# Inverse FFT with its twiddle in the last stage's tables, a 64-bit conversion on three engines, and spare banks for the first batch

## The chip, the cores and the metric

The kernel runs on one core of a Trainium2 chip. The metric is the device time of one execution in microseconds; the median of three runs is given. Beside it there is one profiled execution, whose trace gives the time of every instruction on the engines: PE (TensorE, matmuls; its weight loads are shown as PEld), DVE (VectorE), ACT (ScalarE), POOL (GpSimd) and SP (SyncE). SP, ACT and POOL also issue DMAs, each in a queue of its own that works in order.

## What is computed

A block of two layers, in float32 and float64 on the host; x is (8, 3072, 256).

```python
X = np.fft.rfft(x, axis=1)                        # along the sequence
Yr = Xr @ w_r - Xi @ w_i + b_r                    # complex mixing, 256 x 256
Yi = Xr @ w_i + Xi @ w_r + b_i
Yr = np.sign(Yr) * np.maximum(np.abs(Yr) - 0.01, 0.0)   # Yi likewise
y = np.fft.irfft(Yr + 1j * Yi, n=3072, axis=1)    # (8, 3072, 256)
h = y.reshape(-1, 256) @ w_in                     # 256 -> 2048
g = h * np.tanh(np.log1p(np.exp(np.minimum(h, 20.0))))  # Mish
out = g @ w_out                                   # 2048 -> 256
```

`w_in` and `w_out` come as float64. Nearly every matrix is split into a high and a low part, and a product is made of three matmuls: high by high, low by high, high by low.

## The kernel before

Each batch goes through a chain of four stages, which `chain` (L690) lists as segments of items; between the stages the data lie in DRAM scratch (`scratch`, L310: `s1`, `s3`, `s2`).

- Stage a (`item_a`, 13 items): loads x, splits it, multiplies with the constant table `fa`, forms sum and difference of two halves on DVE into a tile `ev` and stores it to `s1`. The store is issued from ACT's queue (L353).
- Stage b/m (12 blocks; `item_b`, then `item_m`): a block loads 256 KB from `s1` (L365) and a table `tt`, finishes the forward transform (`psb`), splits the result into `xh` and `xl`, multiplies it with the mixing weights (`psm` in the first batch; `psk` and `psp` in the others), thresholds it on DVE (L447) and stores `y` to `s3`. For blocks 0 to 10 a matmul of 256 columns gives two halves, which an ACT copy (`cor`, L414) and a DVE addition (`xf`, L415) add up, in two banks one after the other.
- Stage c (`item_c`, 13 items): loads rows of `s3` in four DMAs of 60 KB, two of them from POOL's queue (`get2`, L582), splits them, multiplies by the inverse transform of length 12 with its twiddle factors, which differ from group to group: 26 tables in seven loads of 450 KB a batch (`cload`, L597). Six matmuls of 256 columns, one ACT copy, a store to `s2` from ACT's queue.
- Stage f (`item_f`, 12 items, two to each chunk of 512 columns): loads 256 KB of `s2` in two DMAs of 64 rows (L657), multiplies by the constant table `vv`, adds, and leaves `yh` and `yl` for the FFN.

The FFN works through 48 chunks with 16 steps each: `ffn1` (L748, six matmuls into `hp`, then Mish on ACT), `split_g` (L763, on DVE for two steps at once: `gh`, `gl`) and, four steps behind (`LAG`), `ffn2` (L771, twelve matmuls into two accumulators `acc`). The chain of batch b+1 is woven into the FFN of batch b: the loop at L868 makes one FFN step and then lets `run_chain` make one step of the chain, or of an f item of the present batch (L884). The first batch has no FFN beside it: its chain runs alone (L844), and only the conversion of the weights runs with it.

That conversion (`from_double`, L224) turns 64-bit numbers into a high and a low part: 16 jobs (`SetupWin`, `SetupWout`) of 512 KB each. A job has nine steps, five tensor_scalars and two scalar_tensor_tensors on DVE, a copy on ACT, and two additions, on POOL in the first half of the start and on DVE later (`aux_eng`). `aux_steps` puts them between the items: 14 jobs ahead of the FFN, two (`N_LATE`) in its first steps.

The order of the work is the order in which the program writes it. `run_chain` (L705) loads `la` items ahead, prepares (splits) `pla` items ahead and then calls the item's matmuls. Buffers come from pools in turn: four load tiles (and, in the first batch, four more of `p_h`), two `ev` tiles, two 4 KB tiles for tables in `p_t`. The eight banks of PSUM are two for `hp`, two for everything in the chain (`ps_d`) and four for the accumulators (`ps_o`).

Of the kernel before, what the change touches and what calls it, by code (L numbers as in the profile page):

```python
# [18 lines left out]
SEQ = 3072  # L19
# [8 lines left out]
def _dft_constants():  # L28
# [42 lines left out]
    u = np.zeros((26, 120, 120))  # L71
    b = np.arange(12)
    for g in range(26):
        nj = 5 if g < 25 else 2
        for j in range(nj):
            k1 = 5 * g + j + 1
            for k2 in range(12):
                th = ang(k1 + 256 * k2, b)
# [7 lines left out]
    cr, ci = 48 + 2 * b, 48 + 2 * b + 1  # L86
    for k2 in range(6):
        th = ang(128 + 256 * k2, b)
        u[25, 48 + 2 * k2, ci], u[25, 49 + 2 * k2, ci] = 2 * np.cos(th), -2 * np.sin(th)
        if k2 < 5:  # L90
            th = ang(256 * (k2 + 1), b)
            u[25, 60 + 2 * k2, cr], u[25, 61 + 2 * k2, cr] = 2 * np.cos(th), -2 * np.sin(th)
    u[25, 70, cr] = np.where(b % 2, -1.0, 1.0)
    u[25, 71, cr] = 1.0

    v = np.zeros((2, 64, 2, 128))
    aa = np.arange(128)
    for s in range(127):
        th = 2.0 * np.pi * (((s + 1) * aa) % 256) / 256
        v[0, s // 2, s % 2], v[1, s // 2, s % 2] = 2 * np.cos(th) / n, -2 * np.sin(th) / n  # L100
    v[0, 63, 1], v[1, 63, 1] = 1.0 / n, np.where(aa % 2, -1.0, 1.0) / n
    v = v.reshape(128, 2, 128)
# [12 lines left out]
def constants():  # L115
# [5 lines left out]
    u = np.concatenate([u, np.zeros((2,) + u.shape[1:], np.float32)])  # L121
    u = u.reshape(7, 4, 120, 2, 120).transpose(0, 2, 1, 3, 4)
    v = np.stack(_hi_lo(v), 2)
# [4 lines left out]
def fft_mix_ffn_kernel(ctx: ExitStack, tc: tile.TileContext, x, w_r, w_i, b_r, b_i, w_in, w_out,  # L128
# [10 lines left out]
    p_t = ctx.enter_context(tc.tile_pool(name="p_t", bufs=2))  # L139
    p_y = ctx.enter_context(tc.tile_pool(name="p_y", bufs=2))  # L140
    p_h = ctx.enter_context(tc.tile_pool(name="p_h", bufs=4))
# [9 lines left out]
    vv = const.tile([128, 2, 2, 128], F32R, name="vv")  # L151
# [9 lines left out]
    u_scr = dramc.tile([7, 120, 4, 2, 120], F32, name="u_scr")  # L161
# [4 lines left out]
    n_ld = [0]  # L166

    def ld_tile(b=1):
        n_ld[0] += 1
        if b == 0 and n_ld[0] % 2:  # L170
            return p_h.tile([128, 512], F32, tag="h", name="ldh")
        return p_ld.tile([128, 512], F32, tag="ld", name="ld")

# [18 lines left out]

    mixraw = []
# [18 lines left out]
    def setup_v():  # L212
        nc.gpsimd.dma_start(out=vv, in_=c_v)

    def copy_consts(n):

        if n < 11:
            nc.sync.dma_start(out=t_scr[n], in_=c_t[n])
        else:
            nc.sync.dma_start(out=t0_scr, in_=c_t0)  # L220
        if n < 7:
            nc.sync.dma_start(out=u_scr[n], in_=c_u[n])

    def from_double(raw, hi, lo, two, t):  # L224


        rv = raw.bitcast(I32).rearrange("p a f -> p (a f)")
        words = rv.rearrange("p (k c w) -> p k c w" if two else "p (c w) -> p c w", w=2, **({"k": 2} if two else {}))
        low, high = (words[:, :, :, n] if two else words[:, :, n] for n in range(2))
        cc = f32(high)  # L230
        if two:
            t = t.rearrange("p (k c) -> p k c", k=2)
        ti = t.bitcast(I32)
        nc.vector.tensor_scalar(out=ti, in0=high, scalar1=0x7FFFFFFF, scalar2=None, op0=ALU.bitwise_and)
        yield
        nc.vector.tensor_scalar(out=t, in0=t, scalar1=E_MIN, scalar2=E_MAX, op0=ALU.max, op1=ALU.min)
        yield
        nc.vector.tensor_scalar(out=ti, in0=ti, scalar1=4, scalar2=1,
                                op0=ALU.logical_shift_left, op1=ALU.logical_shift_right)
        yield  # L240
        nc.vector.tensor_scalar(out=ti, in0=ti, scalar1=0x40000000, scalar2=None, op0=ALU.bitwise_xor)
        yield
        nc.vector.scalar_tensor_tensor(out=ti, in0=high, scalar=-0x80000000, in1=ti,
                                       op0=ALU.bitwise_and, op1=ALU.bitwise_or)
        nc.scalar.activation(out=hi, in_=t, func=ACTF.Copy)
        yield
        nc.vector.tensor_scalar(out=high, in0=ti, scalar1=-0x800000, scalar2=None, op0=ALU.bitwise_and)
        yield
        nc.vector.scalar_tensor_tensor(out=cc, in0=cc, scalar=2.0 ** -52, in1=low.bitcast(U32),
                                       op0=ALU.mult, op1=ALU.mult)  # L250
        yield
        eng = aux_eng[0]
        eng.tensor_tensor(out=t, in0=t, in1=f32(hi), op=ALU.subtract)
        yield
        eng.tensor_tensor(out=lo, in0=cc, in1=t, op=ALU.add)
        yield

    aux_eng = [nc.gpsimd]

    def dt_tile(n):  # L260
        if n is None:
            return p_z.tile([128, 512], F32, tag="y", name="dt")
        return p_y.tile([128, 2, 512], F32, tag=("yh", "yl")[n % 2], name="dt")[:, 0, :]

    N_LATE = 2

    def late(n):
        return n >= 8 - N_LATE

    def raw_tile(n):  # L270
        if n >= 8:
# [657 lines left out]
```

## Time and profile before

| | |
|---|---|
| median of three runs | 2962.04 us (2954.77 to 2965.49) |
| the profiled execution | 2962.3 us, its span 2960.5 us |
| PE busy | 2780.4 us, 94% |
| DVE busy | 1898.4 us, 64% |
| ACT busy | 950.3 us, 32% |
| POOL busy | 171.8 us, 6% |
| mean granted clock of PE | 0.977 |
| DMA | 273.88 MB, 93 GB/s |

Shares are of the span. Busy time of an engine counts the time in which at least one of its instructions runs; issuing a DMA is not counted. A wait in the list of waits reads "engine, tile, line <- what ended the wait: us in total, times, the longest". In the chain of waits a row is a start, a length and what the time went to; a row that names a DMA is a transfer for which somebody waited. In a group of instructions the numbers behind the bar are busy us and the mean ns of one.

### The profile page before, as it was taken

What the parts mean: (1) busy time and instruction counts of PE and PEld (TensorE: products, weight loads), DVE (VectorE), ACT (ScalarE), POOL (GpSimd) and SP (SyncE); (2) the same over time, 40 slices, a digit from 0 to 9 for tenths busy, and PEclk for the clock granted to TensorE, in tenths of its full rate; (3) what the DMA queues carried; (4) which work ended last, traced back from release to release, by engine and by line L of the source; (5) the groups of instructions that cost most, each with busy time, mean ns of one, the idle gap of its engine ahead of it and who ended that gap; (6) DMA issues with size and microseconds to landing.
All of it is one profiled execution on the core that took longest, in us unless ns stands there. A gap on an engine that the chain in (4) does not pass through costs nothing.

```text
span 2960.5 us, 47048 instructions
## 1 busy us (share of the span) xinstructions
PE 2780.4 (94%) x18344; PEld 2549.5 (86%) x18344; DVE 1898.4 (64%) x3222; ACT 950.3 (32%) x1914; POOL 171.8 (6%) x268
## 2 busy tenths in 40 slices
PE   2647999999999999999999999999999999999999
PEld 2536899988999899998999989998999889999998
DVE  4667676566765677566765677656775667654443
ACT  2223333323333333323333233333333233332222
POOL 1230001000020000100010000100002000100000
PEclk9967999999999999999999999999999999999999
DMA  5474233432242322522234322423225222330000
GB/s 157 119 178 138 92 111 103 117 101 72 78 120 81 113 68 61 156 82 78 82 90 123 101 75 75 120 83 109 70 60 162 82 73 82 92 110 29 15 26 15
DMA packets 189399, 273.88 MB, mean 93 GB/s; under 512 B 27711, under 2 KB 114963, under 8 KB 188873
## 3 DMA queue, kind: packets, MB, share of 16 engines
q1 hardware_dynamic: 129745, 190.32, 21.1%
q10 hardware_dynamic: 40088, 50.34, 5.7%
q0 software_dynamic: 19344, 30.21, 4.1%
q8 instruction: 144, 2.36, 0.3%
q14 instruction: 78, 0.64, 0.1%
HBM read 170.03 MB, written 107.31 MB: 94 GB/s over the span
## 4 chain that ended last, share of the span: by engine, by line
PE 83%; DMA 8%; DVE 5%; issue 2%; SPq 1%; ACT 1%; ACTq 0%; DVEq 0%
PE acc L784 34%; PE hp L756 33%; DMA ld<-s 5%; PE psp L493 4%; PE psc L631 2%; PE psf L675 2%; PE psk L474 2%; PE psa L346 2%; PE psb L409 2%; DMA s<-ev 1%; PE psm L510 1%; DMA ld<-in_x_dram 1%; DVE lo L179 1%; PE psf L676 1%; PE psb L411 1%
## 5 line engine op out<-in xcount | busy, mean ns | idle before, releaser
L784 PE MATMUL acc<-wout,gh 128*128 128x256 f32 x6144 | 1144.4, 285 | 0.0
L756 PE MATMUL hp<-yh,win 128*128 128x512 f32 x3072 | 1090.4, 395 | 3.2 <-ACT yh L684 3.2
L784 PEld LDWEIGHTS acc<-wout,gh 128*128 128x128 f32 x6144 | 964.9, 190 | 20.3
L761 ACT ACTIVATE s<-hp 128x512 f32<-128x512 f32 x768 | 459.0, 598 | 1508.6 <-PE hp L756 1351.3
L784 PE MATMUL acc<-wout,gl 128*128 128x256 f32 x3072 | 871.9, 284 | 0.0
L756 PEld LDWEIGHTS hp<-yh,win 128*128 128x128 f32 x3072 | 582.8, 190 | 102.6 <-ACT yh L684 3.4
L756 PE MATMUL hp<-yl,win 128*128 128x512 f32 x1536 | 607.4, 395 | 0.0
L784 PEld LDWEIGHTS acc<-wout,gl 128*128 128x128 f32 x3072 | 582.7, 190 | 0.0
L768 DVE TENSOR_TENSOR gl<-s,gh 128x1024 fp32r<-128x1024 f32 x384 | 472.5, 1230 | 65.1 <-PE acc L784 29.3
L767 DVE CAST gh<-s 128x1024 fp32r<-128x1024 f32 x384 | 264.6, 689 | 324.2 <-ACT s L761 324.1
L756 PEld LDWEIGHTS hp<-yl,win 128*128 128x128 f32 x1536 | 291.5, 190 | 36.0 <-DVE yl L685 0.4
L179 DVE TENSOR_TENSOR lo<-ld,hi 128x512 fp32r<-128x512 f32 (+3 forms) x383 | 263.4, 688 | 46.4 <-ACT hi L178 31.8
L585 POOL DMA_DIRECT2D ld<-s x184 | 109.7, 605 | 2066.6 <-DMA ld<-s 1233.6
L176 DVE CAST hi<-ld 128x512 fp32r<-128x512 f32 (+3 forms) x362 | 150.3, 415 | 83.7 <-DMA ld<-s 62.2
L679 DVE TENSOR_TENSOR eo<-psf,cor 128x256 f32<-128x256 f32 x192 | 77.4, 422 | 173.8 <-ACT cor L678 173.0
L675 PE MATMUL psf<-vv,hi 128*128 128x256 f32 x384 | 100.2, 333 | 43.9 <-DVE sm L433 21.0
L631 PE MATMUL psc<-hi,uu 120*120 120x256 f32 (+1 forms) x416 | 100.7, 303 | 38.3 <-ACT ev L633 26.2
L346 PE MATMUL psa<-hi,fa 120*120 120x256 f32 (+1 forms) x416 | 100.8, 303 | 35.0 <-DVE ev L351 25.1
L493 PE MATMUL psp<-wmix,xh 128*128 128x256 f32 x672 | 133.1, 282 | 0.0
L675 PEld LDWEIGHTS psf<-vv,hi 128*128 128x128 f32 x384 | 74.0, 193 | 53.1 <-ACT s L761 21.8
L448 DVE TENSOR_TENSOR y<-psp,y 128x512 f32<-128x512 f32 x84 | 58.0, 690 | 92.7 <-PE psp L493 92.7
L631 PEld LDWEIGHTS psc<-hi,uu 120*120 120x120 f32 (+1 forms) x416 | 74.4, 196 | 46.4 <-ACT ev L633 29.3
(106 smaller groups left out, 2685.7 us busy)
## 6 DMA issues: line engine op xcount, KB each, us to landing
s<-ev ACTq DMA_DIRECT2D x192, 240.0 KB
out_dram<-ot SPq DMA_DIRECT2D x48, 512.0 KB
ld<-s SPq DMA_DIRECT2D x90, 256.0 KB
ld<-s SPq DMA_DIRECT2D x180, 128.0 KB
s<-y SPq DMA_DIRECT2D x352, 64.0 KB
uu<-u_scr SPq DMA_DIRECT2D x49, 450.0 KB
ld<-in_x_dram SPq DMA_DIRECT2D x180, 120.0 KB
tt<-t_scr SPq DMA_DIRECT2D x66, 256.0 KB
```

Source lines behind the costliest of these rows:

```text
L176: nc.vector.tensor_copy(out=hi, in_=src)
L179: nc.vector.tensor_tensor(out=lo, in0=src, in1=f32(hi), op=ALU.subtract)
L346: nc.tensor.matmul(out=ps[:K, sl], lhsT=fa[:K, h, s, :K], rhs=m[:K, sl], start=n == 0, stop=n == 2)
L493: nc.tensor.matmul(out=it.ps[:, ri * 256:(ri + 1) * 256], lhsT=m[:, c, 130 - ri * 128:258 - ri * 128], rhs=wmix[:, c, s, 2 * ri, :], start ...
L585: eng.dma_start(out=t[p:p + n, g * 256:(g + 1) * 256], in_=rows(k, nrow))
L631: nc.tensor.matmul(out=ps[sl], lhsT=u_t[pr // 2][:K, 2 * (pr % 2) + g, s, :K], rhs=m[sl], start=n == 0, stop=n == 2)
L675: nc.tensor.matmul(out=ps[:, p], lhsT=it.hi[:, q:q + 128], rhs=vv[:, p], start=True, stop=False)
L756: nc.tensor.matmul(out=hp, lhsT=win[:, k, s, f * 128:(f + 1) * 128], rhs=m[:, k, :], start=n == 0, stop=n == 5)
L761: nc.scalar.activation(out=s_t[t // 2][:, t % 2, :], in_=hp, func=ACTF.Mish)
L767: nc.vector.tensor_copy(out=gh, in_=s)
L768: nc.vector.tensor_tensor(out=gl, in0=s, in1=f32(gh), op=ALU.subtract)
L784: nc.tensor.matmul(out=p, lhsT=m[:, t % 2, o:o + 128], rhs=wout[:, f, s, :], start=f == 0 and h == 0 and n == 0, stop=last and h == 1 and ...
```

## The change

1. The twiddle factors of the inverse transform move from the tables of stage c to those of stage f. Stage c then has one table for all groups (three variants, `uu`, loaded once), its groups take rows in steps of two so that an item is one block of 512 columns, and three matmuls of 512 columns take the place of six of 256. Stage f has a table of its own for each item (`it.v`, 256 KB, 12 a batch), loaded by `cload`. `s3` is laid out with even and odd rows apart and `s2` like `s1`; an f item's load is one DMA and all four loads of a c item go through SP's queue.
2. The conversion is cut into three parts. DVE has five operations a job (one in `first`, four in `second`), ACT two copies, POOL the clamp of the exponent, a subtraction, a multiplication and an addition. Ten jobs instead of 14 lie ahead of the FFN, six in its first 17 steps, two program steps in each.
3. The first batch takes its load tiles, `ev` tiles and banks in turn from pools that the FFN uses later (`ld_tile`, `ev_tile`, `ps_tile`), while `started` is false: seven load tiles, five `ev` tiles, all eight banks. In the first batch blocks 0 to 10 of stage b add three matmuls of 128 columns into one bank, as block 11 did, and need no `cor` and no `xf`.
4. In all batches `ps_d` has three banks and `ps_o` three, tables have four tiles of 2 KB, and the `s1` store of stage a goes from ACT's queue to SP's.

```diff
+    uu = const.tile([120, 3, 2, 120], F32R, name="uu")
-    ps_d = ctx.enter_context(tc.tile_pool(name="ps_d", bufs=2, space=PSUM))
-    ps_o = ctx.enter_context(tc.tile_pool(name="ps_o", bufs=4, space=PSUM))
+    ps_d = ctx.enter_context(tc.tile_pool(name="ps_d", bufs=3, space=PSUM))
+    ps_o = ctx.enter_context(tc.tile_pool(name="ps_o", bufs=3, space=PSUM))
...
+    def ld_tile():
+        if not started[0] and turn("ld", 7) in (1, 3, 5):
+            return p_s.tile([128, 2, 512], F32, tag="s", name="lds")[:, 0, :]
         return p_ld.tile([128, 512], F32, tag="ld", name="ld")
+    def ev_tile():
+        if not started[0] and turn("ev", 5) in (1, 2, 4):
+            return p_g.tile([128, 2, 512], F32, tag="gh", name="evg")[:, 0, :]
+        return p_ev.tile([128, 512], F32, tag="ev", name="ev")
+    def ps_tile(name):
+        k = 0 if started[0] else turn("ps", 8)
+        if k in (1, 4, 7):
+            return ps_o.tile([128, 512], F32, tag="o", name=name)
+        if k in (2, 5):
+            return ps_h.tile([128, 512], F32, tag="h", name=name)
+        return ps_d.tile([128, 512], F32, tag="d", name=name)
...
+        def first(self):
+            self.t = p_dt.tile([128, 2, 256], F32, tag="dt", name="dt")
+            nc.vector.tensor_scalar(out=self.t.bitcast(I32), in0=self.high, scalar1=0x7FFFFFFF, scalar2=None,
+                                    op0=ALU.bitwise_and)
+            nc.gpsimd.tensor_scalar(out=self.t, in0=self.t, scalar1=E_MIN, scalar2=E_MAX, op0=ALU.max, op1=ALU.min)
+        def second(self):
...
+            nc.vector.tensor_scalar(out=ti, in0=ti, scalar1=4, scalar2=1,
+                                    op0=ALU.logical_shift_left, op1=ALU.logical_shift_right)
+            yield
+            nc.vector.tensor_scalar(out=ti, in0=ti, scalar1=0x40000000, scalar2=None, op0=ALU.bitwise_xor)
+            yield
+            nc.vector.scalar_tensor_tensor(out=ti, in0=high, scalar=-0x80000000, in1=ti,
+                                           op0=ALU.bitwise_and, op1=ALU.bitwise_or)
+            yield
+            nc.vector.tensor_scalar(out=high, in0=ti, scalar1=-0x800000, scalar2=None, op0=ALU.bitwise_and)
+            yield
+        def third(self):
+            cc, lowf = f32(self.high), f32(self.low)
+            nc.scalar.activation(out=self.hi, in_=self.t, func=ACTF.Copy)
+            nc.scalar.activation(out=lowf, in_=self.low.bitcast(U32), func=ACTF.Copy, scale=2.0 ** -52)
+            nc.gpsimd.tensor_tensor(out=self.t, in0=self.t, in1=f32(self.hi), op=ALU.subtract)
+            nc.gpsimd.tensor_tensor(out=cc, in0=cc, in1=lowf, op=ALU.mult)
+            nc.gpsimd.tensor_tensor(out=self.lo, in0=cc, in1=self.t, op=ALU.add)
+    N_EARLY = 10
...
-            nc.scalar.dma_start(out=s1[5 * pr:5 * pr + J].rearrange("j m c -> (j m) c"), in_=ev[:K])
+            nc.sync.dma_start(out=s1[5 * pr:5 * pr + J].rearrange("j m c -> (j m) c"), in_=ev[:K])
...
-            if blk == 11:
-                ps = ps_d.tile([128, 2, 256], F32, tag="d", name="psb")
+            if blk == 11 or b == 0:
+                ps = ps_tile("psb").rearrange("p (c i) -> p c i", c=2)
...
+                                nc.tensor.matmul(out=ps[:, c].rearrange("p (r e i) -> p e r i", r=2, e=2)[:, e],
+                                                 lhsT=m[:, o:o + 128],
+                                                 rhs=it.tt[0][:, e, s].rearrange("p (r i) -> p r i", r=2),
+                                                 start=n == 0, stop=n == 5)
...
+            ps = ps_tile("psc")
+            for g in range(1 if pr < 12 else 2):
+                sl = slice(0, 512) if pr < 12 else slice(g * 256, (g + 1) * 256)
+                var = 0 if pr < 12 else 1 + g
                 for n, (s, m) in enumerate(((0, it.hi), (0, it.lo), (1, it.hi))):
-                    nc.tensor.matmul(out=ps[sl], lhsT=u_t[pr // 2][:K, 2 * (pr % 2) + g, s, :K], rhs=m[sl], start=n == 0, stop=n == 2)
+                    nc.tensor.matmul(out=ps[:K, sl], lhsT=uu[:K, var, s, :K], rhs=m[:K, sl], start=n == 0, stop=n == 2)
...
-            for ri in range(2):
-                nc.sync.dma_start(out=it.t[64 * ri:64 * ri + 64].rearrange("q (p c) -> q p c", p=2),
-                                  in_=s2[:, 2 * nb + ri, :].rearrange("(q p) c -> q p c", p=2))
+            nc.sync.dma_start(out=it.t, in_=s2.rearrange("q m c -> m q c")[2 * nb:2 * nb + 2])
+        def cload():
+            it.v = p_t.tile([128, 2, 2, 128], F32R, tag="t", name="vt")
+            if b == 0:
+                nc.gpsimd.dma_start(out=it.v, in_=c_v[nb])
+            else:
+                nc.sync.dma_start(out=f32(it.v), in_=v_scr[nb])
...
-        segs.append([item_c(b, p) for p in (*range(8), 12, *range(8, 12))])
+        segs.append([item_c(b, p) for p in (12, *range(12))])
...
+        PACE = (1, 0.6, 1, 3)
-        for k in run_chain(first, la=6, cla=4, on_seg=on_seg):
+        for k in run_chain(first, la=6, cla=3, on_seg=on_seg):
...
-            if 1 <= t <= 15:
-                aux_steps(3)
+            if t < 17:
+                aux_steps(2)
```

`PACE` is the number of conversion steps for each step of the chain, by segment. At the borders of the segments three, five and eight steps are made at once.

More of the change, by code (lines that the diff above doesn't have):

```diff
@@ L191, in setup_dft, with setup_u @@
         nc.gpsimd.dma_start(out=fa, in_=c_fa)
+    def setup_u():
+        nc.gpsimd.dma_start(out=uu, in_=c_u)
     mixraw = []
@@ L220, in copy_consts @@
             nc.sync.dma_start(out=t0_scr, in_=c_t0)
[L221 to L256, printed above, removed]
@@ new lines, in fft_mix_ffn_kernel, with weight_jobs, w1, w2 @@
+    N_EARLY = 10
+    def weight_jobs():
+        def w1(k, n):
+            sl = slice(n * 512, (n + 1) * 512)
+            return (w_in.bitcast(I32)[k * 128:(k + 1) * 128, n * 1024:(n + 1) * 1024],
+                    *(win[:, k, s, sl].rearrange("p (a c) -> p a c", a=2) for s in range(2)), False)
+        def w2(n):
+            return (w_out.bitcast(I32)[n * 256:(n + 1) * 256, :].rearrange("(k p) c -> p k c", p=128),
+                    *(wout[:, 2 * n:2 * n + 2, s, :] for s in range(2)), True)
+        order = [w1(0, 0), w1(1, 0), w1(0, 1), w1(1, 1), w2(0), w2(1), w1(0, 2), w1(1, 2), w2(2), w2(3),
+                 w1(0, 3), w1(1, 3), w2(4), w2(5), w2(6), w2(7)]
+        return [FromDouble(n, *a) for n, a in enumerate(order)]
@@ L341, in mm @@
         def mm():
-            ps = ps_d.tile([128, 512], F32, tag="d", name="psa")
+            ps = ps_tile("psa")
             for h in range(2):
@@ L359, in item_b @@
         it = Item()
+        it.tt = []
         def load():
[L362 removed]
+            it.t = ld_tile()
             s1 = scratch(b)[0]
@@ L504, in mm_c @@
             if c == 0:
-                it.ps = ps_d.tile([128, 512], F32, tag="d", name="psm")
+                it.ps = ps_tile("psm")
             xh, xl = src.x
@@ L800, in fft_mix_ffn_kernel @@
         setup_dft()
-        aux = [SetupWin(k, n) for n in range(4) for k in range(2)] + [SetupWout(n) for n in range(8)]
+        aux = weight_jobs()
         n_raw = [0]
@@ L808, in aux_load @@
                 n_raw[0] += 1
-        N_EARLY = len(aux) - N_LATE
         def aux_run():
+            aux_load(3)
+            aux[0].first()
+            yield
             for n, job in enumerate(aux):
-                aux_load(n + 1)
-                for _ in job.work():
-                    yield n
-                aux_load(min(n + 4, N_EARLY) if n < N_EARLY else n + 4)
+                if n:
+                    aux[n - 1].third()
+                aux_load(n + (3 if n + 3 > N_EARLY else 4))
+                yield from job.second()
+                if n + 1 < len(aux):
+                    aux[n + 1].first()
+                yield
+            aux[-1].third()
         aux_gen = aux_run()
         n_aux = [0]
-        started = [False]
         def aux_steps(m):
             for _ in range(m):
-                if n_aux[0] < 9 * (len(aux) if started[0] else N_EARLY):
+                if started[0] or n_aux[0] < 5 * N_EARLY + 2:
                     next(aux_gen, None)
```

275 lines of the change are left out of this document (101 added, 174 removed).

## The prediction

> **What bounds the kernel now.** I read the page first, then busy time in windows cut at the stage borders of the first batch, then the waits of PE, then the chain of waits and the time line inside each stage.
>
> ```profile
> span 2960.5 us, 47048 instructions
> ...
> PE 2780.4 (94%) x18344; PEld 2549.5 (86%) x18344; DVE 1898.4 (64%) x3222; ACT 950.3 (32%) x1914; POOL 171.8 (6%) x268
> ```
>
> ```profile
> 0.00:63.05 63.05, 20.89 (x78) 17.19 (x78) 27.91 (x56) 16.65 (x34) 10.86 (x18) 1.00 0.52 163
> 63.05:172.73 109.68, 61.31 (x250) 48.66 (x250) 71.63 (x139) 27.65 (x58) 26.06 (x29) 0.93 0.45 123
> 172.73:233.38 60.65, 22.16 (x78) 17.53 (x78) 33.98 (x63) 19.38 (x35) 18.60 (x31) 0.50 0.74 190
> 233.38:245.17 11.79, 4.31 (x17) 3.64 (x17) 5.09 (x12) 3.87 (x9) 0.00 (x0) 0.50 0.40 126
> 245.17:275.72 30.55, 24.13 (x117) 20.10 (x118) 28.50 (x46) 8.51 (x16) 6.60 (x6) 0.84 0.33 100
> 275.72:2700.00 2424.28, 2391.91 (x16145) 2209.16 (x16145) 1619.69 (x2762) 803.92 (x1639) 109.63 (x185) 0.99 0.32 94
> 2700.00:2960.50 260.50, 255.67 (x1663) 233.23 (x1661) 111.60 (x150) 70.28 (x125) 0.00 (x0) 1.00 0.06 20
> ```
>
> The columns of the windows are length, busy time (and instructions) of PE, PEld, DVE, ACT and POOL, granted clock, DMA share, GB/s. The borders are the first b load (63.05), the first c load (172.73), the first f load (233.38), the first FFN matmul (245.17), and the end of the last long PE gap of the start (275.72). From there PE is the bound: 2391.91 of 2424.28 busy, 32.4 us idle. Before it lie 245 us in which the first batch has the chip alone and PE works 109 of them, and 30.6 us in which the FFN starts while DVE is busy 28.50. So a change to the steady part can win at most the 32.4 us and what it takes off PE; the larger store is the 275.7 us.
>
> The profiled execution took 2962.3 us, its span 2960.5, so 1.8 us lie around it; the median of the runs is 2962.04. I sum against 2962.3.
>
> **Steady part.** PE's waits from 276 us on are all of one kind:
>
> ```profile
> PE psf L675 <- DVE sm L433: 21.0, 7, 3.0
> PE psf L675 <- DVE ev L351: 7.5, 6, 1.5
> ```
>
> An f item takes two banks of `ps_d`, which has two. When a b item of block 11 (it keeps its bank until `sm` is made) or an a item (until `ev`) stands before it, the second `psf` waits for that bank. With three banks the second `psf` finds one free: 21.0 + 7.5 = 28.5 us are at stake. What is late next in f is its own `lo`, the rest of the 32.4. I take 25 off; ends: 32 (all), 10 (if PE only runs into the next bank). The bank comes from the output accumulators, which go from four to three: a chunk then takes its second bank from the previous chunk's first accumulator. ACT copies that right behind its last matmul, and between lie the other accumulator, an FFN1 step and one more accumulator: about 0.7 + 1.4 + 0.7 us of matmuls by the rows below. I cost it at 0; if ACT came 2 us later in each of 47 changes of chunk, half of that would be lost.
>
> ```profile
> 282.52 1.39 PE hp L756 x6
> 283.91 0.71 PE psa L346 x6
> 284.62 1.43 PE acc L784 x12
> ```
>
> The c items' six matmuls of 256 columns become three of 512. Six of 256 take 0.71 us, three of 512 half of 1.39, so 0.02 us for twelve items in seven batches: 2 us. Wider matmuls and half the weight loads bring no more, since the weight loads are hidden. The tables are an exchange: 7 of 450 KB for u against 12 of 256 KB for v in each batch.
>
> ```profile
> 202.28 0.69 SPq L580
> ...
> 234.03 2.60 DMA ldh<-s
> ```
>
> SP takes more: the `s1` stores come from ACT's queue (ACT, and the Mish behind, no longer wait there for `ev`, but PE didn't wait for that), and the c loads that POOL issued. The next x load now stands behind a store that waits for `ev`. An x item has two loads to issue, at some 0.7 us (SPq, above), and a step of the loop lasts 1.39 + 0.71 + 1.43 = 3.5 us, so the queue keeps up but runs less far ahead; who waits then is `hi` on DVE, with `gh` and `gl` of the FFN behind it. FFN2 runs four steps behind FFN1, some 7 us of slack after the cast. I take +4 for all batches, ends 0 and +20.
>
> **The conversion.**
>
> ```profile
> L768 DVE TENSOR_TENSOR gl<-s,gh 128x1024 fp32r<-128x1024 f32 x384 | 472.5, 1230 | 65.1 <-PE acc L784 29.3 <-PE hp L756 0.9
> ...
> L243 DVE SCALAR_TENSOR_TENSOR dt<-raw,dt 128x512 int32<-128x512 int32 x16 | 11.1, 692 | 0.5
> ...
> L253 POOL TENSOR_TENSOR dt<-dt,win 128x512 f32<-128x512 f32 x8 | 10.1, 1266 | 99.5 <-ACT win L245 99.5
> ...
> L238 DVE TENSOR_SCALAR dt<-dt 128x512 int32<-128x512 int32 x16 | 6.9, 431 | 0.5
> ```
>
> ```profile
> 251.31 1.29 POOL L253 TENSOR_TENSOR dt<-dt,wout 128x512 f32<-128x512 f32 x1 [26.42 <-ACT wout L245]
> 251.47 2.21 DVE L768 TENSOR_TENSOR gl<-s,gh 128x1024 fp32r<-128x1024 f32 x1
> ```
>
> A job costs DVE five tensor_scalars like L238 and two operations like L243 now, 5 x 0.43 + 2 x 0.69 = 3.5 us, 4.9 where two more are on DVE. After: 4 x 0.43 + 0.69 = 2.4 in five steps (0.48 each); ACT gets one more copy; POOL gets four operations, three like L253 (1.27) and a clamp that no row shows; the nearest are L238 on DVE (0.43) and L253 itself, and I take 1.3: 5.1 us a job on POOL. And POOL's operations hold DVE up: `gl` took 2.21 beside POOL's 1.29, against 1.23.
>
> **The first batch, stage by stage.**
>
> ```profile
> 34.61 5.04 DMA s<-ev
> ...
> 53.03 4.99 DMA s<-ev
> ```
>
> Stage a: from 34 us on the chain goes through stores of `ev`, the first and the last of three shown, because a third item needs one of two tiles back. With five tiles and eight banks in turn these waits go. Next is the DMA: 63.05 us at 163 GB/s are 10.3 MB, and at 190, the rate of stage c, they take 54 us. The store joins SP behind two more loads, where it delays nothing that isn't already six ahead. 63 to 53: -10; ends -4 and -18.
>
> Stage b/m: the chain goes from one block's `psm` over DVE to the next one's. The first, and two neighbours later:
>
> ```profile
> 84.90 4.67 PE psm L510 x12
> ...
> 134.18 3.06 PE psm L510 x12
> ...
> 140.93 3.06 PE psm L510 x12
> ```
>
> `psm` and two `psb` in turn share two banks, so PE waits for DVE and DVE for PE, 6.75 us a block, 3.7 of them outside `psm`. After the change `psb` is one bank without the ACT copy and the two `xf` adds, and eight banks in turn uncouple the two engines. PE needs 3.06 plus twelve matmuls of 128 columns, no longer than the twelve of `acc` (1.43): 4.5 us. DVE needs `lo`, `xl` and a threshold of two operations and a clamp, priced like L243 (0.69, the same 128x512) and L238 (0.43), and 1.8 steps of conversion (0.6 for each of three yields, at 0.48): 4 x 0.69 + 0.43 + 0.87 = 4.1. With up to 0.8 of hold by POOL it is 4.9. But the b load has a price of its own:
>
> ```profile
> 69.80 5.00 SPq L365 DMA_DIRECT2D ldh<-s  x1
> ```
>
> ```profile
> 70.00:80.00 10.00, 4.38 (x15) 3.56 (x16) 1.99 (x3) 2.04 (x5) 0.00 (x0) 1.00 0.14 53
> ```
>
> While only b loads run, 256 KB take 5.0 us at 53 GB/s with a DMA share of 0.14, about two of 16 engines. Twelve of them can't come faster, and tables, raw weights and stores share those two. So 5.0 is one end of a block and 6.75, as now, the other; I take 5.5, nearer to 5.0 because the loads run three ahead. From first load to first `psm` 22 us as now (63 to 85), eleven blocks of 5.5, a tail of 6: 88 against 109.7, -21; ends -8 and -30.
>
> Stage c: all four loads of an item go to SP.
>
> ```profile
> uu<-in_c_u_dram POOLq DMA_DIRECT2D x7, 450.0 KB, 8.4
> ```
>
> 13 x 4 issues of 0.7 are 36 us, and behind the last come its landing (2.6 as the f load's, above), split, matmuls and copy (some 3) and the last store (up to 5.0 as in stage a): 47. By bytes: 60.65 us at 190 GB/s are 11.5 MB; without 3.15 MB of u tables 8.4 MB, 44 us. So 49, above both, against 60.7: -12; ends -6 and -17.
>
> Stage f: now two DMAs an item, which land in 2.60 us (above). The new single one, (2 rows m, 64 q, 512) into 128 partitions, has word for word the form of the b load, so I price it at 5.0 us and the second behind the first at 10: +5; ends 0 and +8. In the Trainium skill, "DMA: Bandwidth & Descriptors", section "Why a DMA increments its semaphore by 16 and not by 1", the number of engines is the largest up to 16 that divides the slowest dimensions of both sides: 128 and 2 here, so two engines. The trace agrees (share 0.14); without the row I would, by that rule alone, come to the same +5, and by size alone to 0.
>
> **The FFN's opening.** In the stages ahead of the FFN the conversion is covered by the waits above. But 10 instead of 14 jobs come before the FFN, so six instead of two fall into its first 15 steps. There DVE has no room: 28.50 of 30.55 now. Six jobs add 6 x 2.4 = 14 us, and 24 operations at 0 to 1.0 us of hold add 0 to 24. In the steady window DVE is busy 1619.69 of 2424.28, so a third of a step's 3.5 us is free; with the a splits that fall here I take 0.9 us, 13 over 15 steps; a lag of 5 is hidden by FFN2's distance. With half the holds (12): 14 + 12 - 13 - 5 = 8, to be set against the two jobs whose cost is in today's 30.55 and which partly stay. I take +10 for the opening; ends 0 and, with every hold and no lag hidden, 14 + 24 - 13 = +25.
>
> The Trainium skill, "SBUF — State Buffer", section "Who interferes with whom", says that of a DVE operation with two SBUF inputs and a reading GpSimd one the second blocks fully until the first ends. The rows agree (0.98 us lost behind 1.29). By the rule taken strictly, every one of the 24 would block and the opening cost the +25.
>
> **Sum.** a -10, b/m -21, c -12, f +5, opening +10, `psf` waits -25, c columns -2, SP and DMA in the steady part +4: -51. 2962.3 - 51 = 2911. Its own range, with single terms between their ends: 2897 to 2927.
>
> **The rivals.**
> - The start gains more: DVE and PE run b/m at the 4.9 of DVE with the loads ahead (-30), and the opening costs nothing because the pieces fall into DVE's waits for `ld`. 2911 - 9 - 10 = 2892, and 2877 with stage a and the `psf` waits at their ends (-8, -7). For it: DVE is busy 71.63 of 109.68 only. Against: the 5.0 us of a load.
> - DVE and the two engines bind: b/m stays near 6.7 a block (+13) and the opening costs 25 (+15): 2939; with stage a at its own end (-4) 2945. For it: 28.50 of 30.55, 2.21 for `gl`, and 6.75 so near what 5.0 and the shared traffic make.
> - The third bank doesn't do what it says: `psf` still waits, now for the `eo` of its own first half or for DVE lagging behind the x loads: +25, 2936.
> - Slower: the f load in the steady part. Ten f items a batch load with a step distance of about three (10.6 us) to their split on DVE. On two engines the load takes 5.0 alone; with one or two b loads, or x loads, in the same ring ahead it takes 10 to 15, DVE stands still in order, `gh` comes late and PE stops. Below some 7 us of lag nothing is lost. Beyond it, 2 us for each of 70 loads are 140: 3051. It decides the sign from 51/70 = 0.7 us a load on. Against it: DVE already waits for `ld` now, and PE shows nothing of it:
>
> ```profile
> DVE hi L176 <- DMA ld<-s: 54.4, 27, 4.4
> ```
>
> **How the numbers follow.** Forecast 0.46; more gain 0.20; DVE and engines bind 0.20; bank without effect 0.07; slower by the f load 0.07. The range 2877 to 2945 leaves out the slower case, half of the first rival's spread below 2892 at most, and nothing of the second. A measurement of this kernel can tell about 0.5% (15 us) from no change: below 2947 is faster. All but the last rival lie there, the second and third so near the bound that I leave 0.07 of theirs to no change: faster 0.86, same 0.07, slower 0.07.
>
> **What would show it.** In the profile after: first b load at about 53, first c load at 141, first f load at 190, first FFN matmul at 207 us; b loads of 5 us; `psf` waits from there on under 10 us in all; an opening in which DVE is over 90% busy and operations of 1.2 and 0.7 us are stretched beside POOL; PE's steady rate (12 `acc`, 6 `hp`, 6 `psa` in 3.5 us) unchanged. Wrong, if the first FFN matmul comes after 230, if PE waits in the steady part for `acc` or `hp` (accumulator banks, late `gh`), or if `hi` waits for `ld` grow by tens of us and PE with them.

## The result, and the profile after

After the change the kernel takes 3001.43 us (median of 4 runs, 2998.65 to 3006.35), before it 2962.09 us beside it: a ratio of 1.0138, 95% interval 1.0115 to 1.0161. It is slower, by 39 us, where 51 us less were forecast. The profiled execution took 2998.65 us. Its page:

```profile
span 2996.9 us, 45927 instructions
...
PE 2807.7 (94%) x18100; PEld 2535.6 (85%) x18100; DVE 1882.6 (63%) x3141; ACT 931.3 (31%) x1899; POOL 130.6 (4%) x126
```

PE is busy 27 us longer than before although it has 244 matmuls less; part of that is a lower granted clock, as the chunks below show. Now the windows of the first batch, cut at the same events as before: first b load (52.60), first c load (154.15), first f load (206.62), first FFN matmul (231.00), and then the first and second chunk of the FFN.

```profile
0.00:52.60 52.60, 25.63 (x78) 17.94 (x78) 21.11 (x46) 15.11 (x31) 9.73 (x15) 1.00 0.61 189
52.60:154.15 101.55, 64.32 (x294) 52.14 (x294) 62.48 (x96) 20.68 (x41) 38.82 (x38) 0.92 0.42 120
154.15:206.62 52.47, 25.17 (x42) 10.25 (x42) 26.33 (x36) 21.27 (x38) 23.91 (x18) 0.50 0.47 140
206.62:231.00 24.38, 4.67 (x17) 3.71 (x17) 6.44 (x13) 3.65 (x9) 7.78 (x8) 0.50 0.38 117
231.00:303.00 72.00, 58.86 (x323) 50.90 (x324) 62.93 (x97) 23.65 (x46) 36.37 (x27) 0.88 0.38 108
303.00:369.70 66.70, 60.80 (x396) 54.78 (x395) 45.51 (x81) 19.40 (x45) 8.70 (x13) 0.97 0.40 126
```

The stages: a takes 52.6 us (before 63.05), b/m 101.6 (109.7), c 52.5 (60.7), f 24.4 (11.8). The FFN starts 14.2 us earlier than before, not 38. Then its first two chunks take 72.0 and 66.7 us; before they took, by the windows of the same two chunks:

```profile
245.17:307.30 62.13, 55.71 (x322) 49.40 (x323) 53.11 (x93) 18.23 (x36) 6.60 (x6) 0.89 0.39 123
307.30:371.30 64.00, 60.66 (x397) 55.66 (x396) 40.92 (x75) 20.54 (x46) 2.12 (x4) 0.95 0.32 100
```

At the start of the third chunk only 1.6 us of the lead are left (369.7 against 371.3). From there to the end of the span the kernel after needs 2627.2 us and the kernel before 2589.2: the 38 us are lost in the steady part. A batch has six chunks; the chunk in which the a items end and the b items begin is the second, the c items fill the fifth and sixth. One batch in the middle, its second, third and fifth chunk, before:

```profile
1690.80:1753.80 63.00, 59.66 (x396) 54.77 (x395) 40.90 (x75) 20.50 (x46) 0.00 (x0) 0.97 0.20 63
1753.80:1815.05 61.25, 61.25 (x429) 57.12 (x428) 46.40 (x81) 21.92 (x47) 0.00 (x0) 1.00 0.26 78
1876.31:1929.62 53.31, 53.31 (x360) 49.14 (x359) 34.35 (x56) 18.58 (x34) 14.59 (x25) 1.00 0.62 172
```

and after:

```profile
1708.88:1774.59 65.71, 60.14 (x396) 54.57 (x395) 41.44 (x78) 19.43 (x45) 0.00 (x0) 0.97 0.27 84
1774.59:1835.78 61.19, 61.19 (x428) 57.04 (x427) 46.73 (x83) 21.71 (x47) 0.00 (x0) 1.00 0.29 90
1896.96:1952.39 55.43, 53.77 (x337) 47.85 (x335) 30.26 (x49) 16.72 (x32) 0.00 (x0) 1.00 0.38 120
```

The third chunk is as it was. The second is 2.7 us longer and PE idle in it for 5.57 us (3.34 before); in the fifth PE is idle for 1.66 us where it was never idle before. The six middle batches, cut in the same way, show the same: in their mean the first chunk is 1.2 us shorter, the second 2.6 longer, the fifth 3.5 and the sixth 1.2 longer, 6 us a batch. The waits of PE and DVE from 303 us on say for what:

```profile
PE psb L392 <- DVE hi L193: 31.0, 7, 6.1
PE psf L639 <- DVE hi L193: 13.6, 10, 3.8
...
DVE hi L193 <- DMA ld<-s: 279.8, 62, 11.4
```

The `psf` waits for `sm` and `ev` have gone as forecast. In their place stand 44.6 us behind `hi`, and `hi` itself waits 279.8 us for loads from the scratch tensors (62.2 in the whole of the run before). The same batch in the time line of SP, then the rows of DVE and PE that follow:

```profile
1709.36 6.89 SPq L350 DMA_DIRECT2D s<-ev  x4
1716.35 0.36 SPq L623 DMA_DIRECT2D vt<-v_scr  x1
1716.76 0.58 SPq L616 DMA_DIRECT2D ld<-s  x1
1717.44 1.38 SPq L373 DMA_DIRECT2D tt<-t_scr  x3
1718.92 4.88 SPq L363 DMA_DIRECT2D ld<-s  x2
```

```profile
1732.57 0.43 DVE L193 CAST hi<-ld 128x512 fp32r<-128x512 f32 x1 [9.56 <-DMA ld<-s]
...
1733.05 0.79 PE L392 MATMUL psb<-tt,hi 128*128 128x256 f32 x2 [4.26 <-DVE hi L193]
```

SP stands at the four last `s1` stores (L350), then issues the f load (L616) and 2.2 us behind it the first b load (L363). The b load is there 13.7 us after its issue. In the last moments of PE's gap nothing else is at work:

```profile
1731.00:1732.50 1.50, 0.00 (x0) 0.00 (x0) 0.00 (x0) 0.00 (x0) 0.00 (x0) 1.00 0.13 49
```

All engines idle, 0.13 of 16 DMA engines busy, 49 GB/s: two engines' worth of a load that DVE, and PE behind it, wait for.

### The profile page after: what moved, and what is told of

The parts are those of the page before. It is cut to its first block, busy times and chain, and to the rows that moved or that the text cites. A ratio compares the mean times of both kernels' runs of the same rounds, so it can differ in the third digit from the quotient of the medians.

```text
span 2996.9 us, 45927 instructions
## 1 busy us (share of the span) xinstructions
PE 2807.7 (94%) x18100; PEld 2535.6 (85%) x18100; DVE 1882.6 (63%) x3141; ACT 931.3 (31%) x1899; POOL 130.6 (4%) x126
## 4 chain that ended last, share of the span: by engine, by line
PE 67%; DMA 16%; SPq 6%; DVE 5%; issue 4%; POOL 1%; ACT 1%; ACTq 0%; DVEq 0%; POOLq 0%
PE acc L748 27%; PE hp L720 26%; DMA ld<-s 12%; PE psp L491 4%; SPq L577 4%; PE psk L472 2%; DMA ld<-in_x_dram 2%; PE psb L407 2%; PE psa L343 2%; PE psf L639 1%; PE psc L598 1%; DMA lds<-s 1%; DVE lo L196 1%; DVE hi L193 1%; DVE gh L731 1%
## 5 line engine op out<-in xcount | busy, mean ns | idle before, releaser
L193 DVE CAST hi<-ld 120x512 fp32r<-120x512 f32 (+2 forms) x360 | 154.6, 430 | 326.9 <-DMA ld<-s 279.8
L196 DVE TENSOR_TENSOR lo<-ld,hi 120x512 fp32r<-120x512 f32 (+2 forms) x382 | 268.4, 703 | 54.8 <-ACT hi L195 34.8
L639 PE MATMUL psf<-vt,hi 128*128 128x256 f32 x384 | 100.4, 332 | 38.0 <-ACT hi L195 20.5
L643 DVE TENSOR_TENSOR eo<-psf,cor 128x256 f32<-128x256 f32 x192 | 74.7, 419 | 90.0 <-ACT cor L642 89.7
L648 ACT ACTIVATE yh<-yt 128x512 fp32r<-128x512 f32 x96 | 60.7, 632 | 190.1 <-DVE yt L646 190.1
L598 PE MATMUL psc<-hi,uu 120*120 120x512 f32 (+1 forms) x224 | 91.3, 417 | 30.2 <-ACT hi L195 28.2
L639 PEld LDWEIGHTS psf<-vt,hi 128*128 128x128 f32 x384 | 73.8, 192 | 49.0 <-ACT hi L195 21.4
L343 PEld LDWEIGHTS psa<-hi,fa 120*120 120x120 f32 (+1 forms) x416 | 75.8, 199 | 43.6 <-ACT hi L195 24.6
L491 PEld LDWEIGHTS psp<-wmix,xh 128*128 128x128 f32 x672 | 109.0, 188 | 3.6
```

The costliest lines, as they stand in the source:

```text
L193: nc.vector.tensor_copy(out=hi, in_=src)
L196: nc.vector.tensor_tensor(out=lo, in0=src, in1=f32(hi), op=ALU.subtract)
L343: nc.tensor.matmul(out=ps[:K, sl], lhsT=fa[:K, h, s, :K], rhs=m[:K, sl], start=n == 0, stop=n == 2)
L491: nc.tensor.matmul(out=it.ps[:, ri * 256:(ri + 1) * 256], lhsT=m[:, c, 130 - ri * 128:258 - ri * 128], rhs=wmix[:, c, s, 2 * ri, :], start ...
L598: nc.tensor.matmul(out=ps[:K, sl], lhsT=uu[:K, var, s, :K], rhs=m[:K, sl], start=n == 0, stop=n == 2)
L639: nc.tensor.matmul(out=ps[:, p], lhsT=it.hi[:, q:q + 128], rhs=it.v[:, p], start=True, stop=False)
```

## The experiments

The prediction's slower rival was the single f load on two engines. As theory A it stood against theory B (the `s1` stores, moved to SP, hold up the loads behind them) and theory C (SP has too many loads to issue, the c loads above all). Times are given with their ratio to the kernel before on the same chip; the kernel after has 1.0138.

**The f load as two DMAs** of 64 partitions each, else the kernel after:

```diff
-            nc.sync.dma_start(out=it.t, in_=s2.rearrange("q m c -> m q c")[2 * nb:2 * nb + 2])
+            for ri in range(2):
+                nc.sync.dma_start(out=it.t[64 * ri:64 * ri + 64], in_=s2[:, 2 * nb + ri, :])
```

> The kernel after, with each f load issued as two DMAs of 64 partitions instead of one of (2, 64, 512). Theory A (the single f load uses two DMA engines, so it and the b and x loads behind it in the same rings land late, DVE waits in order, PE idles and loses clock): the first f load to the first FFN matmul falls from 24.4 us to about 13, the long `hi` waits of DVE for `ld` (279.8 us in all) fall to near the 62.2 of before, the PE waits `psb` for `hi` and `psf` for `hi` go, and the time falls by 11 + about 35 to 2945 to 2960. Theory B (the s1 stores on SP hold up the x and b loads): only the 11 us of stage f come back, about 2988, and `psb` still waits for `hi`. Theory C (the SP queue as a whole is too full, the c loads above all): two more issues an item make it no better, 2985 to 3005.

Measured: 2936.57 us, 0.9897 (0.9882 to 0.9911). One DMA instead of two made the difference between 1.0% faster and 1.4% slower. Windows of this kernel: stage f, the second and the fifth chunk of the same batch.

```profile
208.07:224.10 16.03, 4.04 (x16) 3.56 (x16) 6.60 (x12) 3.83 (x8) 7.72 (x8) 0.50 0.80 187
1670.52:1732.77 62.25, 59.99 (x396) 54.82 (x395) 40.95 (x76) 19.96 (x46) 0.00 (x0) 0.97 0.29 91
1855.14:1908.40 53.26, 53.26 (x337) 47.87 (x335) 32.81 (x52) 17.96 (x33) 0.00 (x0) 1.00 0.44 131
```

Stage f takes 16.0 us instead of 24.4, the fifth chunk has no idle PE, the second 2.26 us. Theory A holds, and the gain is larger than it said, although its signs came only in part: stage f was to take 13 us, and DVE's waits for `ld` from the scratch tensors were to fall to 62 us and fall to 130.9. It isn't the whole cause, as the next two show.

**The `s1` stores back on ACT's queue**, else the kernel after:

```diff
-            nc.sync.dma_start(out=s1[5 * pr:5 * pr + J].rearrange("j m c -> (j m) c"), in_=ev[:K])
+            nc.scalar.dma_start(out=s1[5 * pr:5 * pr + J].rearrange("j m c -> (j m) c"), in_=ev[:K])
```

> The kernel after, with the s1 stores back on ACT's queue. Theory A (two-engine f load): nearly nothing, 2990 to 3008, since the f load stands ahead of the b loads in the rings all the same. Theory B (stores on SP): the x and b loads are issued earlier and the steady part gives back 20 to 40 us: 2960 to 2980.

Measured: 2968.18 us, 1.0005 (0.9996 to 1.0015). This is theory B's range, outside A's. Windows: stage a, the second and the fifth chunk.

```profile
0.00:58.20 58.20, 25.75 (x78) 17.90 (x78) 20.71 (x47) 15.06 (x31) 9.71 (x15) 1.00 0.57 171
1699.68:1758.51 58.83, 58.10 (x397) 53.33 (x396) 41.20 (x77) 20.16 (x47) 0.00 (x0) 1.00 0.23 73
1880.87:1938.92 58.05, 55.30 (x336) 49.21 (x335) 31.58 (x50) 17.63 (x33) 0.00 (x0) 0.97 0.39 119
```

The second chunk loses its gap (58.8 us, 0.73 idle), with the f load as slow as ever; the fifth keeps it. SP's time line of this kernel tells why:

```profile
1688.16 0.42 SPq L623 DMA_DIRECT2D vt<-v_scr  x1
1688.70 0.58 SPq L616 DMA_DIRECT2D ld<-s  x1
1689.86 3.21 SPq L373 DMA_DIRECT2D tt<-t_scr  x3
1708.87 1.14 SPq L363 DMA_DIRECT2D ld<-s  x2
```

The f load is issued 20 us ahead of the b load and is over when that starts, which has landed by 1716.81 (DVE's next `hi`), 7.9 us after its issue instead of 13.7. With stores in the queue SP waits for the last `ev` and then issues both within 2.2 us. So the stores hardly delay the b load's issue (9.2 us into the chunk here, 10.0 in the kernel after): they hold back the f load until it stands right ahead of the b load.

**The second load of each c pair back on POOL**, else the kernel after (`get` has the engine as an argument):

```diff
-                get(12 * m, g, 256 - k1 - 2 * (m - 1), m)
+                get(12 * m, g, 256 - k1 - 2 * (m - 1), m, nc.gpsimd if g or b or pr % 3 else nc.sync)
```

> The kernel after, with the second load of each pair of c loads back on POOL's queue, as before. Theory A (two-engine f load): nearly nothing, 2990 to 3010. Theory C (SP's queue is too full): the c chunks (4 and 5 of a batch) lose their `psf` and `psc` waits for `hi`, 10 to 25 us less: 2975 to 2990.

Measured: 2970.85 us, 1.0011 (1.0001 to 1.0020), below both expectations. Second and fifth chunk:

```profile
1691.35:1756.93 65.58, 60.77 (x396) 55.64 (x395) 41.87 (x79) 19.39 (x45) 0.00 (x0) 0.95 0.28 84
1879.30:1932.56 53.26, 53.26 (x337) 47.87 (x336) 34.00 (x54) 18.19 (x33) 14.93 (x26) 1.00 0.45 131
```

The reverse picture: the second chunk keeps its gap, the fifth loses it. With all c loads on SP the f load is issued 14.8 us into the fifth chunk, here 10.4. The other batches show the same: in the six middle ones the second chunk takes 65 to 67 us in the kernel after, 59 to 61 with the stores on ACT and 65 to 66 here, the fifth 55 to 60, 56 to 59 and 53 to 55. So in the fifth chunk the loss needs two causes at once, the slow f load and the c loads on SP. In the second the slow f load and the stores act together, and taking away the stores gives back more (6.5 us in the mean of these batches) than splitting the load (3.4).

**The kernel before with only its f load made one DMA**, (2, 64, 2, 256) into 128 partitions:

```diff
-            for ri in range(2):
-                nc.sync.dma_start(out=it.t[64 * ri:64 * ri + 64].rearrange("q (p c) -> q p c", p=2),
-                                  in_=s2[:, 2 * nb + ri, :].rearrange("(q p) c -> q p c", p=2))
+            nc.sync.dma_start(out=it.t.rearrange("q (p c) -> q p c", p=2),
+                              in_=s2.rearrange("(q p) m c -> m q p c", p=2)[2 * nb:2 * nb + 2])
```

> The kernel before, with only its f load made one DMA, (2, 64, 2, 256) into 128 partitions, instead of two of 64 partitions. Theory A (two-engine f load): the first f load to the first FFN matmul grows from 11.8 us to 17 to 25, DVE's `hi` waits for `ld` grow from 62 us to 200 or more, PE waits for `hi` at `psb`, and the time goes from 2962 to 2990 to 3010. Theories B and C (stores, SP's queue): only the 5 to 13 us of stage f, 2967 to 2975.

Measured: 2992.75 us, 1.0082 (1.0067 to 1.0097). The one edit makes the old kernel slower by 25 us, as theory A had it. Its stage f takes 20.0 us, and DVE's waits for `ld` between 400 and 2700 us come to 163.2 us (54.4 before). But PE does not wait at `psb` for `hi`, the sign that went with it; its new wait is another:

```profile
DVE hi L176 <- DMA ld<-s: 163.2, 60, 4.8
...
PE psk L474 <- DVE xf L415: 11.6, 7, 2.3
```

This wait lies mostly in the third chunk, which takes 62.9 to 63.2 us in the six middle batches instead of 61.25. The second takes 62.5 to 64.3 us, no more than before (62.8 to 64.7). So the slow f load alone does not make the second chunk's loss.

**Both edits**, the f load split and the stores on ACT:

> The kernel after with both edits: the f load as two DMAs of 64 partitions, the s1 stores on ACT's queue. If the loss in the second chunk of a batch needs both causes (a late f load and stores in SP ahead of the b load), each edit alone has already removed it and what is left there with the f load split (2.5 us idle, 62.6 us long) is the stores: then the chunk falls to about 59, 7 times 3.8 us off the 2936.6 of the split alone: 2905 to 2917. If the stores matter only through the slow f load: no change, 2932 to 2940.

Measured: 2927.13 us, 0.9871 (0.9852 to 0.9890), 10 us above what was expected. The second chunk did fall, to 59.3 us in the same batch, no lower than with the stores on ACT alone (58.8): the split gains nothing there once the f load is out of the b load's way. But the FFN starts 6.2 us later than with the f load split alone (230.3 against 224.1), because stage a ends at 58.0 instead of 52.5. The stores on SP shorten the first batch and lengthen the others.

**And the b loads on more engines**: as the last, and each b load as two DMAs of 64 partitions.

```diff
-            src = s1.rearrange("b m c -> m b c")[2 * blk:2 * blk + 2]
-            nc.sync.dma_start(out=it.t, in_=src)
+            for r in range(2):
+                nc.sync.dma_start(out=it.t[64 * r:64 * r + 64], in_=s1[:, 2 * blk + r, :])
```

> As the run with both edits, and each b load as two DMAs of 64 partitions. If the first batch's b/m stage (101.9 us, 8 under before instead of the 21 forecast) is held by b loads on two engines, it falls by 15 us or more and the time by 10 to 20 against the run with both edits. If it is held by the chain from m store to m store on SP with its DVE steps, the stage and the time stay within 4 us.

Measured: 2885.83 us, 0.9731 (0.9713 to 0.9748): 41 us less than without, twice what was expected. Stage b/m and the second chunk:

```profile
58.00:136.30 78.30, 60.18 (x294) 50.65 (x294) 62.09 (x95) 21.13 (x42) 39.52 (x38) 0.89 0.63 156
1633.17:1690.66 57.49, 57.49 (x396) 53.31 (x395) 41.91 (x77) 21.27 (x48) 0.00 (x0) 1.00 0.27 76
```

The stage falls from 102.3 to 78.3 us, the second chunk to 57.49 with no idle time at all. So the two-engine b loads held the stage, not the chain of m stores, and the second chunk still had 2 us to give.

**The kernel after with only the b loads split**, to see what the slow f load does when the b loads are no longer of its form:

> The kernel after with only its b loads as two DMAs of 64 partitions; the f load stays one DMA. If in the second chunk of a batch the f load hurts through the b loads behind it in the same two rings, that chunk's idle time falls from 5 us to 2 or less with the f load still slow, the c chunks keep their 1 to 4 us, and the first b/m stage falls as it did beside the split f load: 2935 to 2955. If the f load itself is what DVE waits for in both places, the second chunk keeps its 5 us: 2960 to 2975, the first batch's gain alone.

Measured: 2945.27 us, 0.9925 (0.9910 to 0.9939). Second and fifth chunk:

```profile
1670.07:1729.83 59.76, 58.02 (x397) 53.29 (x396) 42.62 (x80) 20.06 (x46) 0.00 (x0) 1.00 0.35 95
1852.19:1908.84 56.65, 54.10 (x337) 47.96 (x336) 30.00 (x48) 16.54 (x31) 0.00 (x0) 1.00 0.39 117
```

In the second chunk the idle time is 1.7 us instead of 5.6: there the f load hurts through the b loads behind it. In the fifth 2.6 us remain: there the f load itself is late, issued among the c loads.

**The kernel before with only the b loads split:**

> The kernel before with only its b loads as two DMAs of 64 partitions. If the two shared banks bound the b/m stage before (6.75 us a block, the chain from `psm` to `psm`), little comes of it: 2955 to 2967. If the two-engine load bound it already, the stage gives 15 us or more and the time 2930 to 2950.

Measured: 2916.61 us, 0.9835 (0.9815 to 0.9855), better than either expectation, and for a reason in neither. Stage b/m, then the second chunk, then the two waits of PE and DVE between 400 and 2700 us that were read in the prediction:

```profile
62.90:168.50 105.60, 63.00 (x250) 50.32 (x250) 71.08 (x137) 27.23 (x58) 26.49 (x29) 0.91 0.49 128
1661.64:1719.59 57.95, 57.80 (x396) 53.24 (x395) 40.83 (x75) 20.45 (x46) 0.00 (x0) 1.00 0.24 69
```

```profile
PE psf L675 <- DVE ev L351: 7.9, 6, 2.0
...
DVE hi L176 <- DMA ld<-s: 3.4, 7, 1.0
```

The stage gives 4 us only, so before the change its loads did not hold it; that its two banks did, as read, fits but was not tried alone. But in the second chunk of each batch 5 to 7 us go, with two banks for the DFT as ever: the `psf` waits for `sm` are no longer there, those for `ev` are.

**Two banks again**, in the kernel with all f and b loads split and the stores on ACT:

```diff
-    ps_d = ctx.enter_context(tc.tile_pool(name="ps_d", bufs=3, space=PSUM))
-    ps_o = ctx.enter_context(tc.tile_pool(name="ps_o", bufs=3, space=PSUM))
+    ps_d = ctx.enter_context(tc.tile_pool(name="ps_d", bufs=2, space=PSUM))
+    ps_o = ctx.enter_context(tc.tile_pool(name="ps_o", bufs=4, space=PSUM))
```

> As the run with all loads on 16 engines (f and b loads as two DMAs each, s1 stores on ACT), but with two banks for the DFT and four for the FFN accumulators, as before the change. If the third bank is worth the forecast 25 us, the `psf` waits for `sm` and `ev` come back in each batch (3.3 us idle in the second chunk at a lower clock, 1 in the first) and the time goes from 2885.8 to 2906 to 2918. If an f item's second half waits for something else anyway: within 5 us of 2885.8.

Measured: 2904.18 us, 0.9788 (0.9771 to 0.9804): 18 us more than with three, some below what was expected. The second chunk stays at 57.93, the first goes from 54.64 to 55.78 (`psf` for `ev`); `sm` doesn't come back.

**14 of 16 conversion jobs ahead of the FFN**, on the kernel with the f load split and the stores on ACT:

```diff
-    N_EARLY = 10
+    N_EARLY = 14
...
-        PACE = (1, 0.6, 1, 3)
+        PACE = (1, 1.2, 1, 3)
```

> As the run with both edits, but 14 of the 16 conversion jobs before the FFN instead of 10 (1.2 steps for each yield of the b/m stage instead of 0.6). If the six late jobs and their POOL operations beside DVE make the FFN's opening long (first chunk 74 us, 62 before), the first chunk falls to 62 to 65, and the time by 5 to 10 where the b/m stage hides the four jobs, by 0 where it grows by what the opening saves.

Measured: 2913.13 us, 0.9822 (0.9807 to 0.9838), 14 us less than without, more than the 5 to 10 expected. Stage b/m and the FFN's first chunk:

```profile
58.20:173.90 115.70, 69.13 (x294) 57.61 (x294) 80.32 (x114) 27.08 (x51) 67.28 (x61) 0.87 0.44 124
238.30:296.00 57.70, 54.34 (x323) 48.44 (x324) 49.14 (x84) 18.65 (x38) 14.49 (x13) 0.91 0.48 138
```

The first chunk falls from 74.7 to 57.7 us, lower than before the change; the b/m stage pays 13 us for it, of which the stages behind it give back 5 (the FFN starts 8.0 us later), and the FFN's second chunk gives 5 more.

**The second c loads on POOL**, on the same base:

> As the run with both edits, and the second load of each pair of c loads on POOL's queue as before. If the first batch's c stage is held by 52 issues of 0.7 us on SP, it falls by 5 to 15 us and the time by 4 to 12; the later batches, whose c chunks already run at PE's pace (53.3 and 49.8 us) once the f load is split, gain nothing. If the stage is held elsewhere: within 4 us.

Measured: 2919.08 us, 0.9849 (0.9825 to 0.9872), 8 us less than without. Stage c falls from 53.3 to 45.7 us; its issues on SP did bound it.

**All together**: f and b loads split, 14 early jobs, second c loads on POOL, and the stores on ACT; then the same with the stores on SP in the first batch alone.

> As the run with all loads on 16 engines, and 14 conversion jobs before the FFN, and the second c loads on POOL's queue. If the three stages' savings are separate (the opening's 17 us back at no more than 8 in b/m, c's 5 to 8), 2885.8 falls to 2865 to 2876. If the b/m stage, now short, has no room for four more jobs, it grows by what the opening saves: 2876 to 2888.

> As that, with the s1 stores on SP in the first batch alone (ACT has the conversion and the hi casts there) and on ACT after. If the store on SP is what shortened stage a in the kernel after (52.6 us against 58.0 with the stores on ACT), 3 to 6 us less than that run; if the b loads are what counts there, within 2 us of it.

Measured: 2870.73 us, 0.9675 (0.9659 to 0.9691), and 2865.40 us, 0.9658 (0.9638 to 0.9677). Both lie in their expected ranges, the second with the stores on SP in the first batch as what shortens stage a (52.6 us again). It is the fastest kernel of all, 136 us under the kernel after. Its FFN starts at 207.5 us, and from the second chunk on, at 264 us, PE is busy in 2594.3 of 2599.0 us:

```profile
264.00:2863.00 2599.00, 2594.30 (x17350) 2384.81 (x17348) 1703.34 (x2851) 861.14 (x1738) 118.86 (x199) 1.00 0.31 89
```

## Why the prediction was wrong

**The step that failed** is the one that set the steady part's price for SP and DMA at +4, and with it the sentence against the slower rival: "DVE already waits for `ld` now, and PE shows nothing of it". PE did show it. The row `psf` for `sm`, 21.0 us, was read as a bank that is missing; but `sm` was late because DVE was late, and DVE was late because it stood at `hi` for a b load. In the batch shown above, before the change:

```profile
1713.29 0.43 DVE L176 CAST hi<-ld 128x512 fp32r<-128x512 f32 x1 [4.26 <-DMA ld<-s]
...
1718.55 0.42 DVE L433 TENSOR_TENSOR sm<-psb,sm 128x256 f32<-128x256 f32 x1
```

```profile
1719.12 0.36 PE L675 MATMUL psf<-vv,hi 128*128 128x256 f32 x1 [3.00 <-DVE sm L433]
```

With b loads on more engines that row is gone while the banks are still two. So where a and b meet there was no slack of 7 us left. The slower f load alone still did not lengthen that place, as the kernel before with the one-DMA load shows; the stores on SP, which line the f load up ahead of the b load, made it PE's time. That is also the other way round than the rival had it, where the f load stands behind the b loads.

The forecast change of the span was -51 us and the measured one +36.4. Of the 87 us between them 61 lie in the steady part (-23 forecast, +38 measured from the third chunk on), 13 in stage b/m, 8 in stage f, 4 in stage c and 3 in the opening. The slower rival had a chance of 0.07; its sign (`hi` waits for `ld` that grow by tens of us, and PE with them) is what the profile shows. By the split of the f load alone the spans differ by 62 us (2996.9 and 2934.8): 8 up to the third chunk, 54 in the steady part. That is 0.8 us for each of 70 loads, beyond the 0.7 from which the rival was said to decide the sign, though not its 2 us, and not spread over all loads: it falls on the edge between a and b, and on the f loads among the c loads.

The working also took each of the change's moves on the queue by itself: the store behind `ev` "where it delays nothing that isn't already six ahead" and the c loads as issue time. With a fast f load the c loads on SP are harmless in the steady part (the fifth chunk has no idle PE), and the stores cost 2.6 us a batch in the second chunk (62.62 us in the mean of the six middle batches with them on SP, 60.05 on ACT). What they do is to move the slow load in time, next to what it can hurt: the b load in the second chunk, its own use in the fifth.

Point by point, the other terms:

- Stage a, -10: measured -10.4 (63.05 to 52.60). Right in size by luck, half right in cause: with the stores on ACT it is 58.2, so 5.6 of the 10.4 come from the store's move to SP, which was priced at nothing. The rest is left for the tiles, the banks and the shorter conversion, which no run tells apart.
- Stage b/m, -21: measured -8, its bad end. The work of a block was not too low: with fast loads the whole stage takes 78.3 us, below the 88 forecast. The load was wrong: 5.0 us was its price alone, and in the stage it has other transfers beside it. One b load on the chain of waits of the kernel after:

```profile
124.52 13.23 DMA ld<-s
```

- Stage c, -12: -8.2. The issues on SP were the bound, as worked out. They took 42.5 us instead of 36 (54 of them, with waits between), and what follows the last of them 10, near the 11 of the sum.
- Stage f, +5: +12.6. The split of the load gives back 8 of these; the rest, 16.0 against 11.8, is not settled (the first f load there took some 7 us to its use, with tables, raw weights and x loads on the way).
- The opening, +10: +9.9 in the first chunk and 2.7 in the second, so right in its net size. The parts are not those of the sum: with the f load split and the stores on ACT, the first chunk takes 57.7 us with only two late jobs, 4.4 less than before, and the four others add 17.0. The Trainium skill's rule ("SBUF — State Buffer", section "Who interferes with whom"), read strictly as a full hold for each of the 24 operations, gave +25; that is more than came. In the first chunk DVE's operations are stretched by some 16 us in all beside 22 operations of POOL (an estimate from their lengths there and in the batches without POOL, such as `gh` with 1.12 against 0.69 us and `gl` with 1.63 against 1.23), between the 12 of the half holds and the 24 of full ones. The clamp on POOL, for which no row stood before, was taken at 1.3 us and takes 2.02:

```profile
L265 POOL TENSOR_SCALAR dt<-dt 128x512 f32<-128x512 f32 x16 | 32.3, 2018 | 159.8 <-DVE dt L263 159.8
```

- The `psf` waits, -25: the waits for `sm` and `ev` went. But the row was only in part the bank's: with fast b loads alone the kernel before loses the waits for `sm` and 51 us in all, with two banks. What the third bank adds once the loads are fast is 18 us, opening included, and it takes away the waits for `ev`; those for `sm` are gone without it.
- The c columns, -2: some -0.6 (with the f load split the two c chunks go from 53.31 to 53.26 and from 49.82 to 49.78, times seven).

With its f load left as two DMAs the kernel after is 1.0% faster than before, not the 1.7% forecast.

## What to carry to other kernels

A wait that names a compute operation is not yet explained: follow that operation's own engine back to what *it* stood at, since "bank not free" and "load late" give the same row. Price a DMA by its shape (outermost dimension 2 or 64) and by what else of that shape is on its way at the same time, not by its bytes alone; here the same 256 KB as two DMAs of 64 partitions were worth some 65 us (f) and 41 us (b). And when a change moves a store that waits onto the queue of the loads, ask what it lines up behind itself: two loads that were 20 us apart came to be 2 us apart.

## What the runs showed of the hardware

- One DMA of (2 rows, 64, 512) into 128 partitions moves at 49 GB/s with 0.13 of the 16 engines busy when nothing else is at work, about two of them. The Trainium skill's rule on the number of engines ("DMA: Bandwidth & Descriptors", section "Why a DMA increments its semaphore by 16 and not by 1") agrees. The runs add that such loads take their time one after the other: two b loads of the kernel before, issued 0.6 us apart, are used 5.4 us apart (the second is the `hi` at 1713.29 above), and in the kernel after a b load is used 13.7 us after its issue with an f load issued 2.2 us ahead, against 7.9 us where the f load is long over.
- PE's idle time costs more than itself: the second chunk takes 57.49 us without a gap (all loads split), 63.00 with 3.34 us idle (before) and 65.71 with 5.57 (after). Of the 8.2 us in the last case 2.65 are PE busy longer, at a granted clock of 0.97 instead of 1.00. One gap of 1.69 us, here of the kernel with the f load split, is followed by 5 us at a granted clock of 0.66 (the second row is a window):

```profile
1697.01 0.38 PE L640 MATMUL psf<-vt,hi 128*128 128x256 f32 x1 [1.69 <-DVE hi L193]
```

```profile
1698.00:1703.00 5.00, 5.00 (x26) 4.74 (x26) 4.00 (x11) 1.75 (x6) 0.00 (x0) 0.66 0.14 53
```
